# Backward attention: the token-major K, Q and dO of the next group are requested in four column pieces of 64 KB each instead of one piece of 256 KB

## The chip, the cores and the metric

One core of a Trainium2 chip runs the whole kernel. The metric is the time of one execution on the device in microseconds (us), taken as the median over several executions; less is better. The kernel before has a median of 2633.72 us over 6 runs, which lie between 2625.1 and 2644.07 us. One further thing is needed to read the profile: it is taken from a single execution, and everything in it is counted from the start of that execution's span.

## The reference, cut to what matters

The kernel computes a transformer block (layer norm with modulation, softmax attention with 32 heads of 16 columns over 2048 tokens, a squared-ReLU MLP) and the gradients of all its inputs. The change lies in the backward pass of the attention alone. For one head, the forward pass is

```python
scores = jnp.einsum('bhqd,bhkd->bhqk', q, k) * scale
p = _softmax(scores, axis=-1)
o = jnp.einsum('bhqk,bhkd->bhqd', p, v)
```

and its backward pass, with dO the gradient that arrives at o, needs for each head P = softmax(QK^T) again, dP = dO V^T, dS = P * (dP - rowsum(dO * o)), and then dV = P^T dO, dK = dS^T Q and dQ = dS K. Everything is in bfloat16 with float32 accumulation.

## The kernel before, in words

The program has three stretches: the forward pass with the MLP and its gradients, the backward attention (`attn_bwd`, from L1335), and a last phase (`phase6`) with the remaining weight gradients. The backward attention is the middle one that matters here.

**Groups, halves, slots.** The 32 heads are handled as 8 groups of 4 heads (loop over `g`, L1434). Each group has two halves of 2 heads, which the code calls pairs (loop over `jp`, L1435). A half runs over 4 chunks of 512 keys (`c`) and, in each, over 16 blocks of 128 queries (`ib`), in steps of four blocks (`ib0`, L1452). Such a step of four blocks is called a slot here: its number in the half is `m` (L1453), 0 to 15, so there are 16 slots in a half and 256 in all.

**What a block does.** For each of the two heads, TensorE computes a score tile `st` (L1468), ScalarE takes its exponential into `pu` (L1472), TensorE computes `dp` (L1408) and VectorE multiplies both into `ds` (L1410). `kv` (L1365) accumulates dK and dV from `ds`, `pu` and the group's token-major Q and dO. For dQ the tile `ds` has to be transposed. Of the 32 squares of 128x128 in a slot, TensorE turns the first four (L1427, copied to `dsT` by ScalarE at L1428), and one DMA transpose, issued on SyncE's queue at L1418 when the slot's last `ds` is ready, turns the other 28. `dq` (L1387) multiplies `dsT` with the group's token-major K. It is called two blocks at a time, some two slots behind: it starts on a slot when more than 8 blocks are waiting (L1480). There are four `dsT` buffers and three `ds` buffers.

**What a group loads.** A group needs five tensors of its own, kept in two sets of buffers that alternate: QT and dOT (feature-major) and K, Q and dO (token-major, 128 partitions by 1024 columns, that is 2 KB in each partition and 256 KB in all). `load_group(g)` (L1304) makes the list of copies for them, the *pieces*; from group 2 on QT and dOT come in four pieces each (16 rows of 4 KB, 64 KB; 18 rows of 4 KB, 72 KB), for group 1 in two of 256 KB each. `pair_pieces` (L1327) makes four more for each half: the rows of K and V of the two heads of the next half (two of 64 KB, two of 72 KB). Group 0's pieces are issued before the backward attention starts, on SyncE's queue (L908), followed there by the four copies of `WmT`, which only `phase6` reads.

**When a piece is issued.** While group g is computed, GpSimd's queue issues the pieces of group g+1. The first half takes the four pieces of its own second half and the first half of the list of `load_group`, the second half takes the four of the next group and the rest (L1441 to L1444):

```python
pieces = self.pair_pieces(g, 1) + later[:len(later) // 2]
later = later[len(later) // 2:]
...
pieces = self.pair_pieces(g + 1, 0) + later
```

They are spread evenly over the 16 slots, each behind a copy of one element of the last `ds` (`tick`), which holds GpSimd back until the kernel has come that far (L1454 to L1457):

```python
while pieces and (total - len(pieces)) * SC * ST <= m * G * total:
    if last:
        nc.gpsimd.tensor_copy(tick[:], last[7][0:1, 0, 0, 0:1])
    nc.gpsimd.dma_start(*pieces.pop(0))
```

For the groups 2 to 7 the list of `load_group` has 4 + 4 + 3 = 11 pieces. So a first half issues 4 + 5 = 9 pieces (K and V of the next half, the four of QT, one of dOT), in the slots 0, 2, 4, 6, 8, 9, 11, 13 and 15. A second half issues 4 + 6 = 10 (K and V, three of dOT, then K, Q and dO whole), in the slots 0, 2, 4, 5, 7, 8, 10, 12, 13 and 15: the three pieces of 256 KB are the last three. For group 1 the list has 7 pieces, and the halves issue 7 and 8. The order of the instructions on TensorE, SyncE and GpSimd is the order of the code in this stretch (a manual schedule).

Of the kernel before, what the change touches and what calls it, by code (L numbers as in the profile page):

```python
# [25 lines left out]
def chunks(total, size):  # L26
    out = []
    s = 0
    while s < total:
        w = min(size, total - s)  # L30
        out.append((s, w))
        s += w
    return out
# [72 lines left out]
class K:  # L106
# [1197 lines left out]
    def load_group(self, g):  # L1304

        S, ST, qp = self.S, self.ST, self.qp
        tm = {"K": self.ktm_d, "Q": self.qtm_d, "dO": self.dOp_d}
        fm = {"QT": (self.QTq_d, DH), "dOT": (self.dOTq_d, DH + 2)}
        w = ST * 4 * DH
        if g < 2:  # L1310
            T, o = {}, 0
            for n in (*fm, *tm):
                e = S if n in fm else w
                T[n] = self.q0[:, o:o + e] if g == 0 else qp.tile([P, e], BF16, name=f"{n}g")[:]
                o += e
            self.Tq[g] = T
        T, pieces = self.Tq[g % 2], []
        for n, (src, rows) in fm.items():
            if g < 2:
                pieces += [(T[n][:, s0:s0 + sw], src[g, :, s0:s0 + sw]) for (s0, sw) in chunks(S, 1024)]  # L1320
            else:
                pieces += [(T[n][r:r + rows, :], src[g, r:r + rows, :]) for r in range(0, P, 32)]
        for n, src in tm.items():
            pieces.append((T[n], src[g]))
        return {n: t if n in fm else t.rearrange("p (st w) -> p st w", st=ST) for n, t in T.items()}, pieces

    def pair_pieces(self, g, jp):  # L1327
# [422 lines left out]
```

## Time and profile before

| | us |
|---|---|
| median of 6 runs | 2633.72 |
| lowest and highest | 2625.1, 2644.07 |
| the profiled execution | 2627.91 |
| its span, first to last instruction | 2626.1 |
| backward attention in it, from 1180 to 2490 us | 1310 |

| busy in the span | us | share |
|---|---|---|
| TensorE, matmuls (PE) | 2481.5 | 94% |
| ScalarE (ACT) | 2296.2 | 87% |
| VectorE (DVE) | 1769.6 | 67% |
| GpSimd (POOL) | 513.6 | 20% |

How to read the lines that follow in the prediction: PE is TensorE, PEld its weight load, DVE VectorE, ACT ScalarE, POOL GpSimd, and SPq SyncE's queue. A row of the windows gives a stretch (from:to, us), its length, then each engine's busy us with its number of instructions, the clock that TensorE was granted as a share of full speed, the mean busy share of the 16 DMA engines (packets overlap, so it can exceed 1) and GB/s. A row of the waits says who sat idle until what was done: total us, how often, longest. A row of the DMA queues gives the packets, the MB and the time that the packets took as a share of 16 engines; q1 carries what SyncE issues (here the transposes), q0 what GpSimd issues (here the pieces). A row of the DMA issues gives destination and source, queue, number, KB each and the median us from issue to landing.

### The profile page before, as it was taken

How to read it: one execution, taken by the hardware profiler on the slowest of the kernel's cores; microseconds unless marked ns; L12 is line 12 of the kernel's file. 1: busy time of each engine (PE TensorE's matmuls, PEld its weight loads, DVE VectorE, ACT ScalarE, POOL GpSimd, SP SyncE). 2: the span in 40 equal slices, each digit the busy share in tenths (PEclk: the TensorE clock that was granted, in tenths of full speed). 3: DMA queues.
4: the chain of work that ended last, by engine and by line, in shares of the span. 5: the costliest groups of instructions: out<-in, count | busy, mean ns of one | idle time of the engine just before them, and what ended most of it. 6: DMA issues, size and time to landing. Idle time of an engine off the chain costs nothing.

```text
span 2626.1 us, 77231 instructions
## 1 busy us (share of the span) xinstructions
PE 2481.5 (94%) x31005; PEld 1227.2 (47%) x31233; DVE 1769.6 (67%) x3679; ACT 2296.2 (87%) x3712; POOL 513.6 (20%) x965
## 2 busy tenths in 40 slices
PE   8999899999999999899999999999999999998998
PEld 4555555555555554743434344444443444443443
DVE  6222223323423335659999999999999999998867
ACT  7999999999999995319989999999998999998823
POOL 3545511310321131450000000000000000000031
PEclk9999999999999999999999999999999999999999
DMA  5588742520541246999999999999999999999986
GB/s 165 119 184 189 171 81 95 134 66 22 156 100 43 89 104 187 188 238 187 200 188 194 200 184 194 194 193 201 191 193 190 190 200 196 194 195 197 199 224 169
DMA packets 1192126, 433.47 MB, mean 165 GB/s; under 512 B 1136036, under 2 KB 1158054, under 8 KB 1191766
## 3 DMA queue, kind: packets, MB, share of 16 engines
q1 hardware_dynamic: 1154966, 322.79, 71.8%
q0 software_dynamic: 36800, 105.74, 14.4%
q8 instruction: 244, 4.00, 0.6%
q14 instruction: 116, 0.95, 0.1%
HBM read 75.57 MB, written 68.69 MB: 55 GB/s over the span
## 4 chain that ended last, share of the span: by engine, by line
PE 32%; DMA 23%; ACT 2%; issue 2%; SPq 0%; POOL 0%; DVE 0%; POOLq 0%; ACTq 0%
DMA dsT<-ds 22%; PE st L1468 11%; PE acckv L1365 6%; PE accq L1387 5%; PE dps L1002 2%; ACT pu L1472 2%; PE dps L951 1%; PE dp L1408 1%; PE g3ps L1574 1%; PE dxhps L1549 1%; DMA dqT<-dq_t 1%; PE st L1427 1%; DMA du_blk<-duT_d 1%; PE st L1376 1%; PE gps L1599 0%
## 5 line engine op out<-in xcount | busy, mean ns | idle before, releaser
L1410 DVE TENSOR_TENSOR ds<-dp,pu 128x512 bf16<-128x512 f32 x2048 | 1240.6, 678 | 61.3 <-PE dp L1408 54.3
L1472 ACT ACTIVATE pu<-st 128x512 bf16<-128x512 f32 x2048 | 1081.6, 614 | 124.4 <-PE dp L1408 66.8
L382 ACT ACTIVATE pu<-st 128x1024 bf16<-128x1024 f32 x992 | 912.0, 1078 | 4.5 <-PE st L379 4.1
L379 PE MATMUL st<-QTm,KTq 128*128 128x512 bf16 x1859 | 561.4, 377 | 26.8 <-ACT pu L382 6.0
L313 PEld LDWEIGHTS <-pu 128*128 128x128 bf16 x8192 | 346.8, 96 | 236.0 <-issue 2.8
L1387 PEld LDWEIGHTS <-dsT 128*128 128x128 bf16 x8192 | 245.2, 96 | 268.5 <-issue 207.6
L313 PE MATMUL accbank<-Vaug,pu 128*128 128x17 bf16 x8192 | 358.0, 171 | 8.2 <-ACT Vaug L502 1.1
L1408 PE MATMUL dp<-m,q 64*128 64x512 bf16 x1024 | 342.5, 385 | 0.7 <-DMA WmT<-WmT_d 0.7
L1408 PE MATMUL dp<-m,dOTg 64*128 64x512 bf16 x1024 | 341.5, 384 | 0.0
L1468 PE MATMUL st<-m,q 64*128 64x512 bf16 x1024 | 321.3, 384 | 7.7 <-ACT pu L1472 5.4
L1468 PE MATMUL st<-m,QTg 64*128 64x512 bf16 x1024 | 319.8, 384 | 5.0 <-ACT pu L1472 3.1
L379 PEld LDWEIGHTS <-KTq 128*128 128x128 bf16 x1984 | 188.4, 96 | 177.3 <-issue 126.7
L1456 POOL COPY tick<-ds 1x1 bf16<-1x1 bf16 x142 | 25.1, 176 | 1136.4 <-DVE ds L1410 1136.4
L1387 PE MATMUL accq<-q,dsT 128*128 128x16 bf16 x4096 | 150.2, 171 | 26.8 <-DMA dsT<-ds 26.2
L1387 PE MATMUL accq<-Kg,dsT 128*128 128x16 bf16 x4096 | 150.0, 171 | 26.1 <-DMA dsT<-ds 25.6
L1365 PE MATMUL acckv<-ds,Qg 128*16 128x512 bf16 x1024 | 155.5, 383 | 0.3 <-DVE ds L1410 0.2
L1365 PE MATMUL acckv<-ds,q 128*16 128x512 bf16 x1024 | 155.2, 383 | 0.0
L1365 PE MATMUL acckv<-pu,q 128*16 128x512 bf16 x1024 | 155.2, 384 | 0.0
L1365 PE MATMUL acckv<-pu,dOg 128*16 128x512 bf16 x1024 | 155.1, 383 | 0.0
L1428 ACT COPY dsT<-st 128x512 bf16<-128x512 bf16 x256 | 152.4, 595 | 1.1 <-PE st L1427 1.0
L293 POOL DMA_DIRECT2D QTm<-QTq_d x124 | 63.3, 512 | 335.5 <-PE st L379 314.8
L320 DVE RECIPROCAL rl<-accbank 128x4 f32<-128x4 f32 x128 | 22.9, 179 | 152.9 <-PE accbank L313 152.8
(343 smaller groups left out, 2756.9 us busy)
## 6 DMA issues: line engine op xcount, KB each, us to landing
KTq<-KTq_d POOLq DMA_DIRECT2D x24, 512.0 KB, 3.7
duT_d<-auT POOLq DMA_DIRECT2D x4, 1792.0 KB, 8.8
aT_d<-rT POOLq DMA_DIRECT2D x4, 1792.0 KB, 13.9
KTq_d<-KTq SPq DMA_DIRECT2D x32, 128.0 KB, 2.4
QTq_d<-ev_fm SPq DMA_DIRECT2D x32, 128.0 KB, 2.8
VTq_d<-vT POOLq DMA_DIRECT2D x4, 1024.0 KB, 6.4
O_d<-O POOLq DMA_DIRECT2D x4, 1024.0 KB, 6.4
dsT<-ds SPq DMA_TRANSPOSE x256, 7.8
```

Source lines behind the costliest of these rows:

```text
L293: nc.gpsimd.dma_start(QTm[j][32 * j:32 * j + 32, :], self.QTq_d[g, 32 * j:32 * j + 32, 512 * qc:512 * (qc + 1)])
L313: nc.tensor.matmul(acc[:, a, sub, :], lhsT=pu[:, a, sub * P:(sub + 1) * P], rhs=Vaug[:, kb, h, :], start=(kb == 0 and a == 0 and sub == 0) ...
L379: nc.tensor.matmul(stt[:, a, :], lhsT=KT[:, kb * P:(kb + 1) * P], rhs=QTm[2 * jp + a][:], start=True, stop=True)
L382: nc.scalar.activation(pu[:], stt[:], ACT.Exp, scale=self.scale)
L1002: nc.tensor.matmul(pt[:], lhsT=a[:, st, :], rhs=g_tm[:, st, :], start=(st == 0), stop=(st == ST - 1))
L1365: nc.tensor.matmul(acckv[r:r + DH, :], lhsT=T[n][:, ib, col:col + DH], rhs=src[:, a, :], start=(ib == 0), stop=(ib == ST - 1))
L1387: nc.tensor.matmul(accq[:, ib, a, :], lhsT=dsT[:, (i * 2 + a) * 4 + sub, :], rhs=T["K"][:, 4 * c + sub, col:col + DH], start=(c == 0 and i ...
L1408: nc.tensor.matmul(dp[:], lhsT=T["dOT"][rd, ib * P:(ib + 1) * P], rhs=masked["VT"][2 * jp + a][rd, 512 * c:512 * (c + 1)], start=True, sto ...
L1410: nc.vector.tensor_tensor(dsg[:, i, a], dp[:], pu[:, a, :], ALU.mult)
L1428: nc.scalar.copy(dsT[:, 0:4, :], tp[:])
L1468: nc.tensor.matmul(stt[:], lhsT=T["QT"][rs, q], rhs=masked["KT"][2 * jp + a][rs, c0:c0 + 512], start=True, stop=True)
L1472: nc.scalar.activation(pu[:, a, :], stt[:], ACT.Exp, scale=self.scale)
```

## The change

In `load_group`, each of K, Q and dO is no longer one piece but four, cut along the columns. A piece is 128 partitions by 256 columns, that is 512 B in each partition of the destination and in each row of the source (whose rows stay 2 KB apart), 64 KB in all. One such piece holds four of the 16 token blocks.

```diff
         for n, src in tm.items():
-            pieces.append((T[n], src[g]))
+            pieces += [(T[n][:, a:a + w // 4], src[g, :, a:a + w // 4]) for a in range(0, w, w // 4)]
```

The rest follows from the loop that spreads the pieces. The list of the groups 2 to 7 grows from 11 to 20 pieces, and its middle moves: the first half of a group now issues 4 + 10 = 14 pieces (K and V, four of QT, all four of dOT, two quarters of K) and the second half 4 + 10 = 14 (K and V, two quarters of K, four of Q, four of dO), both in the slots 0, 2, 3, 4, 5, 6, 7, 8, 10, 11, 12, 13, 14 and 15. For group 1 the list grows from 7 to 16 and the halves issue 12 each. Group 0's list grows by the same nine, on SyncE's queue. In all GpSimd issues 63 copies more, each with its one-element `tick`, and SyncE 9 more. Bytes, matmuls and the order of the instructions on TensorE stay as they were.

## The prediction

> **What bounds the kernel now.** I read the chain of waits first: which resource ends last.
>
> ```profile
> DMA dsT<-ds 22%; PE st L1468 11%; PE acckv L1365 6%; PE accq L1387 5%; PE dps L1002 2%; ACT pu L1472 2%; PE dps L951 1%; PE dp L1408 1%; PE g3ps L1574 1%; PE dxhps L1549 1%; DMA dqT<-dq_t 1%; PE st L1427 1%; DMA du_blk<-duT_d 1%; PE st L1376 1%; PE gps L1599 0%
> 1180.00:2490.00 1310.00, 1246.91 (x17600) 534.06 (x17597) 1248.18 (x2063) 1230.42 (x2431) 99.26 (x284) 0.99 1.17 194
> ```
>
> The transpose `dsT` holds 22% of the chain, all of it in the backward attention. The second row is that stretch: TensorE, VectorE and ScalarE are each busy for about 1240 of 1310 us and the DMA share is 1.17. Three engines and the DMA are almost equally full, so a late transfer has little to hide behind. Next the waits of that stretch, then DMA windows of two moments: one transpose with no piece beside it, and one with the 256 KB of Q beside it.
>
> ```profile
> PE accq L1387 <- DMA dsT<-ds: 50.9, 60, 4.6
> ```
>
> ```profile
> q1 hardware_dynamic: 3618, 0.92, 118.4%
> ...
> q1 hardware_dynamic: 1039, 0.27, 74.4%
> q0 software_dynamic: 73, 0.24, 47.8%
> ```
>
> The first q1 row is 1220 to 1224.56 us: 3618 packets (one transpose is 28 squares x 128 rows = 3584) in 4.56 us, against a slot that takes 4.78 us when nothing waits (1333.59 to 1338.37 us, all engines busy throughout). A transpose therefore leaves about 0.2 us of its slot free. The other two rows are 1318 to 1322.5 us: beside Q only 1039 packets pass in 4.5 us. The stage is limited by transposes that arrive late once a piece has been among them; `dq` waits 50.9 us for them.
>
> Where do these waits lie? In the slots 10 to 13 of a second half, where K and Q and then dO are requested, the same row reads, for the groups 0 to 6:
>
> ```profile
> PE accq L1387 <- DMA dsT<-ds: 3.4, 1, 3.4
> ...
> PE accq L1387 <- DMA dsT<-ds: 4.6, 1, 4.6
> ```
>
> shows groups 0 and 4; all seven are 3.4, 2.0, 2.3, 2.4, 4.6, 1.6, 2.0, together 18.3 us. The same slots of the first halves give 0.5 + 0.3 + 0.9 + 0.4 = 2.1 us. So 16.2 us belong to the 21 pieces of 256 KB. The whole halves of group 1:
>
> ```profile
> 1348.20:1427.60 79.40, 77.48 (x1106) 33.55 (x1098) 77.92 (x130) 76.52 (x154) 6.05 (x18) 1.00 1.17 196
> 1427.60:1509.40 81.80, 77.45 (x1110) 33.14 (x1109) 77.77 (x129) 77.41 (x154) 6.94 (x20) 1.00 1.20 195
> ```
>
> VectorE works 77.8 us in either half; the second is 2.4 us longer.
>
> **The change part by part.** *Removed: the 256 KB bursts.* If none of their waiting stays, -16.2 us. Long waits cost a little more: after the 3.4 us of group 0 the slot 1326.76 to 1333.59 us ran at a granted clock of 0.65. The two slots from 1319.48 to 1333.59 us together took 14.11 instead of 9.56, 4.55 more for a wait of 3.4, so 1.1 on top. I leave that to the range.
>
> *Added: 84 pieces of 64 KB* (12 for each of the groups 1 to 7). A small piece is not free: the first halves of groups 1 to 6 wait 0.9 + 4.6 + 3.1 + 2.3 + 2.1 + 1.1 = 14.1 us with 54 pieces, mostly of 64 to 72 KB, 0.26 us each. The slots 0 to 9 of the second halves wait 1.8 + 0.5 + 0.3 + 0.7 + 0.4 + 0.2 = 3.9 us with 42 such pieces, 0.09 us each. Ten of the twelve new pieces fall into second halves, two into first: (10 x 0.09 + 2 x 0.26) / 12 = 0.12 us each, 84 x 0.12 = +10.1 us. Upper bound: all at 0.26, and each packet dearer because its runs are 512 B. For that I compare 512 KB copies of GpSimd's queue with short and longer runs: the store of `dOTq` (512 B runs, 739 to 745 us), then that of `xhat` (1 KB rows, 795 to 801 us).
>
> ```profile
> q0 software_dynamic: 144, 0.52, 29.6%
> ...
> q0 software_dynamic: 144, 0.52, 21.4%
> ```
>
> 29.6 / 21.4 = 1.38 for the same bytes, so 0.26 x 1.38 = 0.36 us and 84 x 0.36 = +30.2 us. These are stores and the pieces are loads, so it is a bound and not my value. Lower bound: nothing, if the pieces fit the free 0.2 us of their slots.
>
> *Moved: three pieces of dOT* per group from the second to the first half (groups 2 to 7): 3 x (0.26 - 0.09) x 6 = +3.1 us; lower bound 0.
>
> *GpSimd:* 63 more copies with ticks.
>
> ```profile
> POOL tick L1456 <- DVE ds L1410: 1136.4, 142, 17.9
> L1457 POOL DMA_DIRECT2D Kg<-ktm_d x4: 551/562/565, 1304.5 to 2294.3; - x4
> ```
>
> 63 x (0.18 for the tick + 0.29 between + 0.55) = 64 us of a queue that waits 1136 us for `ds`. That waiting hides them; queued behind a tick are only later pieces. Were the cover gone, pieces would land late. The nearest deadline is the first quarter of dO, issued in slot 12 and read after slot 15; the landing of whole dO takes 6.3 us (issue rows), three slots are 14 us. The last quarter is issued in slot 15 and read in slot 3. Cost 0.
>
> *SyncE:* nine more issues of 0.43 to 0.57 us before group 0, 4 to 5 us. They delay `WmT`, read only in the last phase, and then the first transpose at 1185.16 us; SyncE was idle from 1170.6 us. Each issue also waits for the copy eight before it, whose landing takes 4 to 5 us, which could move the end of the list to about 1177 us, still 8 us early. Cost 0; without the cover, up to +5.
>
> **Sum:** -16.2 + 10.1 + 3.1 = -3.0 us. The span of 2626.1 becomes 2623.1. The median lies 7.6 us above that span; with this added, 2631 us.
>
> **A rule that speaks against the change.** The page "DMA: Bandwidth & Descriptors" of the Trainium skill, section "Rules for kernel authors", says to coalesce small transfers into a large one, since under 64 KB one pays mostly overhead. Its table in "Bandwidth" has 0.95 us of DMA time for 64 KB and 6.15 us for 1 MB; along a straight line 256 KB would be 1.99 us, so quarters would cost 4 x 0.95 - 1.99 = 1.8 us more for each tensor, an estimate from that page, 38 us for 21 tensors if all of it reached the path. The trace is nearer to neutral: the windows above give 0.09 to 0.26 us of waiting for a small piece and 16.2 / 21 = 0.77 for a large one.
>
> **The rivals.**
>
> *Faster, the pieces fit.* Cut in four, no piece is longer than what two slots leave free, so the waits of 16.2 us go and the new pieces cost next to nothing; the clock stays up (-1.1). 2633.7 - 17 = 2617 us. For it: the wait of the second halves before slot 10 is only 0.09 us per piece. Against it: the first halves, where 64 KB pieces in neighbouring slots do wait.
>
> *Slower, every occupied slot waits.* A transpose fills 4.56 of 4.78 us, so a stage that gets a piece in 28 of 32 slots instead of 19 never catches up. At 0.36 us: -16.2 + 30.2 + 3.1 = +17, 2651 us. The point from which it decides: (16.2 - 3.1) / 84 = 0.16 us for a new piece is break-even, 0.31 us brings a loss of 13 us. For it: the 0.26 us of the first halves and the factor 1.38. Against it: the second halves.
>
> *It changes nothing.* The same bytes take the same DMA time and the waiting only moves. 2634 us. For it: the DMA share is the same in halves with and without large pieces (1.17 to 1.20). Against it: beside Q the total falls to 112 GB/s (1318 to 1322.5 us) from 201 in the window without a piece, so bursts do lose time, not only move it.
>
> **How the numbers follow.** About 0.5%, 13 us, is what a measurement of this kernel can tell from no change; the six runs spread by 19. My sum and "nothing" give one answer, within 0.5%: 0.43 together (0.31 and 0.12). "Fits" gets 0.28: 17 us is just over the bound. "Every slot waits" gets 0.29, since its price rests on rows one step away. The likeliest is the sum, 2631 us; its own range is 2620 (new pieces at nothing: -16.2 + 3.1 = -13) to 2642 (new pieces at 0.26 us: -16.2 + 21.8 + 3.1 = +9). For 8 in 10 I go to the far rivals at either side, with the spread of a median of some runs: 2610 to 2652.
>
> **What would show it.** In the trace after, the slots 10 to 13 of the second halves should wait about as long as those of the first halves, with no single wait over 2 us; if waits of 3 to 4 us remain, the burst was not the cause. The total of `accq` waiting for `dsT` should fall from 50.9 to about 48; 35 means "fits", 65 or more means "every slot waits". The first halves of groups 2 to 7 should grow by about 0.8 us each, the second shrink by 1.0. GpSimd's ticks should still wait over 1000 us, and the first transpose should still be issued near 1185 us. I am wrong in kind if something new waits: TensorE at L1365 for a quarter of Q or dO, or GpSimd for an earlier piece.

## The result, and the profile after

The changed kernel takes 2616.05 us (median of 29 executions, 2602.48 to 2630.95). The kernel before, measured beside it, takes 2633.88 us (66 executions, 2619.39 to 2649.05). The ratio is 0.9932 with a 95% interval of 0.9919 to 0.9946: the change makes the kernel 0.68% faster, 17.8 us. That lies inside the stated range of 2610 to 2652 us, and it is the rival "the pieces fit" (2617 us, given 0.28). The likeliest case of the prediction, 2631 us, had the direction but only 3 of the 17.8 us.

The same views as before, in the same order. First the chain of waits of the changed kernel:

```profile
DMA dsT<-ds 18%; PE st L1468 13%; PE acckv L1365 7%; PE accq L1387 6%; PE dps L1002 2%; ACT pu L1472 2%; PE dp L1408 2%; PE dps L951 1%; PE st L1427 1%; PE g3ps L1574 1%; PE dxhps L1549 1%; DMA dqT<-dq_t 1%; DMA du_blk<-duT_d 1%; PE st L1376 1%; PE gps L1599 0%
```

The transpose gave up 4 points of the chain (22% to 18%), and TensorE's own lines (`st`, `acckv`, `accq`) took them. No new resource appears in it. The waits of the stretch from 1180 to 2490 us (who waited for what: total us, how often, longest us):

```profile
POOL tick L1456 <- DVE ds L1410: 1065.4, 205, 19.4
...
PE accq L1387 <- DMA dsT<-ds: 40.3, 53, 3.8
```

`dq` waits 40.3 us for transposes instead of 50.9. The two windows do not end alike: the last transpose is issued at 2488.1 us before and at 2475.6 after, so only the second window holds the waits behind it. Counted from the first to the last transpose, it is 38.5 us instead of 50.9. GpSimd still stands 1065 us before `ds`, so its 63 additional copies did stay under cover. The same waits in the slots 10 to 13 of the second halves follow. As in the prediction, the slots of a wait are counted by the half's transposes; a piece that the loop puts into its slot m is issued about two transposes earlier. In the second half of group 1 of the kernel before, K, Q and dO, which the loop has in its slots 12, 13 and 15, are issued 10.2, 11.3 and 13.3 transposes into the half. There is one answer for each of the groups 0, 1, 2, 4, 5 and 6 (group 3 has none):

```profile
PE accq L1387 <- DMA dsT<-ds: 0.8, 1, 0.8
...
PE accq L1387 <- DMA dsT<-ds: 0.6, 1, 0.6
...
PE accq L1387 <- DMA dsT<-ds: 1.8, 2, 1.0
...
PE accq L1387 <- DMA dsT<-ds: 0.3, 1, 0.3
...
PE accq L1387 <- DMA dsT<-ds: 0.6, 1, 0.6
...
PE accq L1387 <- DMA dsT<-ds: 0.5, 1, 0.5
```

The sum is 4.6 us, against 18.3 before, and no wait is longer than 1.0 us. The DMA queues of the changed kernel from 1319.5 to 1324 us, a moment with a quarter of dO beside a transpose (packets, MB, share of 16 engines):

```profile
q1 hardware_dynamic: 3512, 0.89, 115.1%
q0 software_dynamic: 32, 0.07, 8.7%
```

Beside the whole Q, 1039 packets of transposes passed in 4.5 us. Beside this quarter 3512 pass, almost the 3584 of one transpose. Five other windows of 4.5 us beside a quarter of dO hold 2322 to 3692; some contain a pause in which hardly anything moves, but none is as slow as beside Q.

Now the halves. A row of the windows is from:to, length, busy us (and instructions) of PE, PEld, DVE, ACT, POOL, then clock, DMA share, GB/s. Group 4 of the kernel before, first and second half:

```profile
1837.00:1917.40 80.40, 77.47 (x1104) 33.41 (x1096) 77.71 (x130) 76.66 (x153) 6.08 (x18) 1.00 1.21 195
1917.40:2002.10 84.70, 78.70 (x1110) 33.64 (x1112) 78.25 (x130) 77.17 (x154) 6.91 (x20) 0.98 1.16 190
```

Groups 1 and 4 of the changed kernel:

```profile
1348.40:1430.60 82.20, 78.62 (x1106) 33.13 (x1104) 78.37 (x130) 77.22 (x153) 9.58 (x28) 0.98 1.19 195
1430.60:1512.30 81.70, 78.85 (x1110) 33.47 (x1112) 78.16 (x130) 77.34 (x154) 9.90 (x28) 0.98 1.15 192
1833.70:1914.00 80.30, 77.52 (x1112) 33.45 (x1104) 77.97 (x130) 76.93 (x153) 9.57 (x28) 1.00 1.20 199
1914.00:1994.40 80.40, 77.00 (x1101) 33.37 (x1096) 77.36 (x129) 76.51 (x152) 9.89 (x28) 1.00 1.23 195
```

In group 4 the second half lost 4.3 us and became as long as the first. GpSimd's column shows the additional pieces: 28 instructions instead of 18 and 20. Group 1 shows why no single half should be read: its two halves are no shorter than before (81.7 against 81.8 for the second), and both ran at a clock of 0.98. One profile moves by several us from half to half, so the table has further profiles of both kernels (b2, a2 and a3 below), and the text uses the means.

Five profiles, in us. "Stage" is from the first to the last transpose `dsT`, "waits" is `accq` waiting for `dsT` in it (a row of waits whose window ends later has up to 2.3 us more), "slots 10–13" is the part of it in those slots of the second halves of groups 0 to 6. The halves are means over groups 1 to 6. "Lost clock" sums, over the stretches of the stage in which the clock was 0.50, half of their length. The last column is TensorE's busy time in the stage.

| | span | stage | waits | slots 10–13 | first half | second half | lost clock | TensorE busy |
|---|---|---|---|---|---|---|---|---|
| before | 2626.1 | 1302.9 | 50.9 | 18.2 | 80.6 | 82.1 | 10.2 | 1240.2 |
| before again (b2) | 2632.2 | 1314.5 | 55.4 | 18.8 | 80.9 | 83.5 | 22.6 | 1246.8 |
| change | 2612.4 | 1292.1 | 38.5 | 4.6 | 80.9 | 80.1 | 8.5 | 1240.2 |
| change again (a2) | 2620.0 | 1289.8 | 37.8 | 1.3 | 81.4 | 79.4 | 6.8 | 1238.5 |
| change, third (a3) | 2609.7 | 1292.2 | 40.0 | 2.7 | 81.6 | 80.0 | 6.8 | 1239.0 |

The mean stage goes from 1308.7 to 1291.4 us. These 17.3 us are about the 17.8 of the medians, so no part outside the backward attention is needed; that they agree so closely is partly luck, since the two profiles of the kernel before differ by 11.6 us. The waits give 53.2 - 38.8 = 14.4 of them. TensorE's busy time for the same matmuls gives 1243.5 - 1239.2 = 4.3, but nearly all of that comes from b2: the first profiles of the two kernels have the same 1240.2. Against it, `st` waits 1.6 us longer for `pu` (means 7.0 and 8.6).

### The profile page after: what moved, and what is told of

Its sections match the earlier page's. It is cut to its first block, busy times and chain, and to the rows that moved or that the text cites. A ratio compares the mean times of both kernels' runs of the same rounds, so it can differ in the third digit from the quotient of the medians.

```text
span 2612.4 us, 77500 instructions
## 1 busy us (share of the span) xinstructions
PE 2477.8 (95%) x31005; PEld 1225.7 (47%) x31233; DVE 1769.3 (68%) x3679; ACT 2296.3 (88%) x3712; POOL 558.5 (21%) x1091
## 4 chain that ended last, share of the span: by engine, by line
PE 35%; DMA 20%; ACT 2%; issue 2%; SPq 0%; POOL 0%; DVE 0%; POOLq 0%; ACTq 0%; DVEq 0%
DMA dsT<-ds 18%; PE st L1468 13%; PE acckv L1365 7%; PE accq L1387 6%; PE dps L1002 2%; ACT pu L1472 2%; PE dp L1408 2%; PE dps L951 1%; PE st L1427 1%; PE g3ps L1574 1%; PE dxhps L1549 1%; DMA dqT<-dq_t 1%; DMA du_blk<-duT_d 1%; PE st L1376 1%; PE gps L1599 0%
## 5 line engine op out<-in xcount | busy, mean ns | idle before, releaser
L1456 POOL COPY tick<-ds 1x1 bf16<-1x1 bf16 x205 | 36.2, 176 | 1065.4 <-DVE ds L1410 1065.4
```

## The experiments

### Both kernels again: what the clock does after a long wait

The kernel before, once more, to see how far its own profile can be trusted:

> The kernel before once more, for a second profile. Its first profile is of an execution of 2627.9 us, 6 us under its median of 2633.9, and has 1302.9 us from the first to the last transpose of ds, 11.5 us more than the mean of three profiles of the change (1291.4), while the medians differ by 17.8 us. If the first profile was a short one of this stage, it takes 1305 to 1312 us here with 53 to 58 us of waits of accq for dsT, and the stage explains the whole difference. If the rest lies elsewhere, it takes 1301 to 1304 us again, and something outside the stage is longer than in the profiles of the change.

It took 2634.01 us in its one execution. Its stage is 11.6 us longer than in the first profile with waits only 4.5 us longer, and TensorE busy for 6.6 us longer; the windows around one of its long waits show where this lies. First the waits from 1290 to 1320 us:

```profile
PE accq L1387 <- DMA dsT<-ds: 4.1, 3, 3.6
```

Then three windows of the same kernel, of which the first holds that wait (columns as above, the third from the right is TensorE's clock):

```profile
1304.00:1312.20 8.20, 5.32 (x76) 2.20 (x73) 6.52 (x11) 5.99 (x12) 0.00 (x0) 1.00 1.26 146
1312.20:1319.00 6.80, 5.83 (x60) 1.80 (x60) 3.38 (x6) 3.61 (x7) 0.72 (x2) 0.50 1.07 222
1319.00:1326.00 7.00, 6.75 (x104) 2.86 (x100) 6.72 (x12) 6.51 (x14) 0.00 (x0) 1.00 0.94 143
```

After the wait the clock is 0.50 for 6.8 us. In these 6.8 us TensorE does 60 matmuls, against 104 in the 7.0 us that follow, and VectorE is busy for half of the time. This comes on top of the wait.

A shorter wait can do it too. In the changed kernel a wait of 1.4 us ends at 1389.4 us; the wait, then three windows:

```profile
PE accq L1387 <- DMA dsT<-ds: 1.4, 1, 1.4
```

```profile
1387.90:1391.10 3.20, 1.80 (x30) 0.74 (x30) 1.96 (x5) 2.30 (x5) 0.00 (x0) 1.00 1.23 254
1391.10:1394.50 3.40, 3.40 (x36) 1.02 (x32) 2.88 (x6) 2.93 (x6) 0.69 (x2) 0.50 1.14 184
1394.50:1397.90 3.40, 3.40 (x59) 1.49 (x56) 3.02 (x6) 2.89 (x6) 0.50 (x2) 1.00 1.30 187
```

At 0.50 there are 36 matmuls in 3.4 us, then 59. Over the five profiles, all 9 waits of `accq` of 3 us or more were followed by a stretch at 0.50, of 3.4 or 6.8 us; so were 12 of the 25 waits of 1.25 to 2 us, always for 3.4 us, 3 of the 5 of 2 to 3 us, and only 4 of the 250 under 1.25 us. The Trainium skill, page "TensorE: Matmul & The Clock Gate", part 1, "What's actually happening", has the clock at half rate after at least one idle window of about 3.4 us. The waits of 3 us and more agree with that; those of 1.25 to 2 us do not, and here the measurement decides.

Of the stretches at 0.50 in the stage, 3 of 5 in the first profile of the kernel before and 5 of 10 in b2 begin in the slots 10 to 13 of the second halves of groups 0 to 6. With the change none does (11 stretches in three profiles), and there no wait in these slots is over 1.0 us. The lost clock is not simply added to the waits: 14.4 us of waits and 9.0 us of clock (means 16.4 and 7.4) together would exceed the 17.3 us. What reaches the stage of it is at most the 4.3 us of TensorE's busy time.

The change again, twice, on the chips of the later experiments:

> The changed kernel once more, beside the others of this call on one chip. Ratio to before 0.9932 as found, within 0.9915 to 0.995. Its own question: the 48 transposes and loads ahead of the backward attention (from the first transpose of du to the first of a) took 92.0 us in the profile of before and 85.9 us in that of the change, and no instruction there differs. If that is chance from run to run, it will lie anywhere from 84 to 97 us here; if it belongs to the kernel, at 86 us.

> The changed kernel as a yardstick for the two others of this call. Ratio to before 0.9925 to 0.9955; waits of accq for dsT 39 to 41 us; first to last transpose of ds 1289 to 1293 us.

Measured: 2622.22 us, ratio 0.9950 [0.9932, 0.9969], and 2616.68 us, 0.9939 [0.9916, 0.9962]. The waits of the stage in a2:

```profile
PE accq L1387 <- DMA dsT<-ds: 39.2, 56, 3.7
```

and in a3:

```profile
PE accq L1387 <- DMA dsT<-ds: 41.7, 61, 3.2
```

So the gain and its place hold in three profiles. Whether a chip gives 0.5 or 0.7% is within the intervals.

### The parts of the change

The change does two things at once: it cuts the copies, and it moves pieces between the halves. The first four experiments take them apart and set a floor.

**e1, the quarters in the old halves.** On the changed kernel, the list is cut where it was cut before (4 of QT and one of dOT in the first half). The second line lets the last slot issue what is left, since a half now has over 16 pieces.

```diff
-pieces = self.pair_pieces(g, 1) + later[:len(later) // 2]
-later = later[len(later) // 2:]
+cut = (5 if g else 3) if g + 1 < NQ else len(later) // 2
+pieces = self.pair_pieces(g, 1) + later[:cut]
+later = later[cut:]
...
-while pieces and (total - len(pieces)) * SC * ST <= m * G * total:
+while pieces and ((total - len(pieces)) * SC * ST <= m * G * total or m == SC * ST // G - 1):
```

> K, Q and dO in quarters, but the list is cut where it was cut before: the first half of a group issues K and V, four of QT and one of dOT (9), the second half three of dOT, all twelve quarters and K and V of the next (19, so three slots issue two). Theory 'burst' (a 256 KB copy among the transposes costs more than its quarters do one by one): most of the gain stays, ratio to before 0.993 to 0.995, waits of accq for dsT some 40 to 43 us. Theory 'room' (the gain is that the second half has fewer bytes to carry, since dOT moved to the first): the gain is gone, ratio 0.998 to 1.002, second halves again about 82 us each.

**e2, whole pieces in the new halves.** On the kernel before, QT and dOT are all in the first half and K, Q and dO, whole, have the second for themselves.

```diff
-pieces = self.pair_pieces(g, 1) + later[:len(later) // 2]
-later = later[len(later) // 2:]
+cut = (8 if g else 4) if g + 1 < NQ else len(later) // 2
+pieces = self.pair_pieces(g, 1) + later[:cut]
+later = later[cut:]
```

> K, Q and dO whole (256 KB), but all of QT and dOT in the first half, so the second half issues only K and V of the next and the three large pieces, in slots 0, 3, 5, 7, 10, 12 and 14. Burst: each large piece still costs its 0.8 us of waiting, ratio 0.998 to 1.001, waits 48 to 52 us, single waits of 3 us or more remain. Room: nearly the whole gain, ratio 0.993 to 0.995.

**e3, no token-major pieces.** As e2, but K, Q and dO are loaded for the groups 0 and 1 alone. This leaves out work that the result needs: the later groups compute with the K, Q and dO that lie in the two sets of buffers.

```diff
-pieces.append((T[n], src[g]))
+if g < 2:
+    pieces.append((T[n], src[g]))
```

> Left out: K, Q and dO of the groups 2 to 7 are not loaded at all (the two sets of buffers keep those of the groups 0 and 1, the output is not the reference's); QT and dOT all in the first half. This is the floor: what all 18 large pieces cost together, against the run with the same halves and whole pieces. Burst: whole pieces cost about 1 us each, quarters nearly nothing, so the floor lies at or just under the changed kernel: ratio 0.990 to 0.993. If quarters cost 0.12 us each as I had it (72 x 0.12 = 9 us), the floor lies 9 us under the changed kernel: ratio 0.989 to 0.990. Room: also 0.990, but then the whole pieces with the new halves are as fast as the change.

**e4, quarters by rows.** The same 64 KB, cut along the partitions, so that each row keeps its 2 KB.

```diff
-pieces.append((T[n], src[g]))
+pieces += [(T[n][r:r + 32, :], src[g, r:r + 32, :]) for r in range(0, P, 32)]
```

> Quarters of 64 KB again, but cut by partitions (32 partitions by 2 KB each, source contiguous) and not by columns (128 partitions by 512 B). Slots and halves as in the changed kernel. If runs of 512 B cost more (the factor 1.38 of the stores), this is faster than the change: ratio 0.989 to 0.991. If only the size of a piece matters, it is the same: 0.992 to 0.995. If what matters is that a piece lies evenly over all partitions, it is slower than the change: 0.996 or more.

| | us | ratio, 95% | stage | waits | slots 10–13 |
|---|---|---|---|---|---|
| e1 | 2616.68 | 0.9945 [0.9922, 0.9967] | 1297.5 | 43.1 | 4.7 |
| e2 | 2630.22 | 0.9987 [0.9963, 1.0012] | 1314.4 | 58.9 | 13.4 |
| e3 | 2607.63 | 0.9917 [0.9886, 0.9948] | 1288.6 | 38.4 | 2.4 |
| e4 | 2624.56 | 0.9983 [0.9959, 1.0006] | 1294.3 | 40.8 | 2.7 |

e1 and e2 settle which part it is. Cutting alone gives the gain, within the intervals; moving alone gives none that can be measured. The waits of e2's stage:

```profile
PE accq L1387 <- DMA dsT<-ds: 58.9, 63, 5.0
```

Whole pieces keep their long waits (5.0 us the longest) wherever the others are put. e3 is the floor. Its 18 whole pieces less than e2 are worth 2630.22 - 2607.63 = 22.6 us, 1.26 us each; the two intervals leave some 10 us on either side of the 22.6. And its waits are

```profile
PE accq L1388 <- DMA dsT<-ds: 40.3, 48, 3.0
```

as long as those of the changed kernel (38.4 us of them in the stage, against 38.8). So waiting of this size is there without any K, Q and dO of the groups 2 to 7. In the time, the floor lies 9.0 us under e1, which ran beside it, and 4.0 under the change by the two ratios; with an interval of 8 us on either side it cannot tell these from nothing.

e4 looked like a contradiction. Its stage is like the change's (1294.3, with 2.7 us in the slots 10 to 13), but its time is not. Its trace differs elsewhere: the stage ahead, between the first transposes of `du_blk` and of `a_blk`, took 96.8 us, where e1, e2 and e3 have 83.5 to 89.4 us and the instructions are the same. It was measured again, beside the change.

> The quarters by rows once more. In its first profile the backward attention was as short as with the change (1294.3 us from first to last transpose of ds, the change 1292.1, before 1302.9), but the stage ahead of it, from the first transpose of du to the first of a, took 96.8 us. If that is chance, the ratio to before now comes down to that of the change, 0.992 to 0.995. If it belongs to this kernel, the ratio stays at 0.997 to 0.999 and the stage near 97 us.

Measured: 2623.2 us, 0.9952 [0.9930, 0.9975], and a2 beside it 0.9950. Its stage is 1292.1 us. So in the backward attention both profiles of e4 are like the change, and in the second measurement so is the time. The first, 0.9983 over 12 executions, stays unexplained: one profile with a long stage ahead does not show that the other executions had one too. That the cut by columns costs more, by its 512 B in each row, is not seen in either.

**e5, every quarter twice.** On the changed kernel, from group 1 on, each quarter is requested a second time: 84 more pieces of 64 KB, which is the marginal price by itself.

```diff
-pieces += [(T[n][:, a:a + w // 4], src[g, :, a:a + w // 4]) for a in range(0, w, w // 4)]
+for a in range(0, w, w // 4):
+    pieces += [(T[n][:, a:a + w // 4], src[g, :, a:a + w // 4])] * (2 if g else 1)
```

(with the second condition of e1 in the loop)

> The price of a quarter by itself: for the groups 1 to 7 each of the twelve quarters is requested twice in a row (the same bytes to the same place), so 84 copies of 64 KB come on top and some slots issue two. Burst with a low price (0.05 us each, as the floor without token-major loads says): 84 x 0.05 = +4 us on the change, ratio to before 0.994 to 0.996. My price of 0.12 us: +10, ratio 0.997. The price of the first halves, 0.26 us: +22, ratio 1.001 or more.

Measured: 2626.48 us, 0.9969 [0.9949, 0.9990]; the change beside it took 2622.22. The difference is 4.3 us for 84 pieces, 0.05 us each. The two intervals together leave about 7 us on either side, so the price lies between nothing and 0.14 us: below the break-even of 0.16, but 0.12 is not excluded. Its one profile is less kind:

```profile
PE accq L1388 <- DMA dsT<-ds: 59.0, 65, 4.0
```

These 59.0 us are 20 more than in a2, beside it, with 20 pieces in the 16 slots of a half, so that some slots have two; they are not all a slot apart. That execution (2633.75 us) was slower than this kernel's median by 7 us. So the times leave the price of a quarter open between nothing and 0.14 us. How the waits of a half grow with its number of pieces, over all runs, is in the next section.

**e7, halves instead of quarters** (`w // 4` becomes `w // 2`, 128 KB each).

> K, Q and dO in two pieces of 128 KB each. If the cost grows with the length of a piece (burst), half of the gain or a bit more: ratio 0.994 to 0.997. If a piece only has to fit into what one or two slots leave free, 128 KB already does: 0.9925 to 0.994, the same as quarters. If it doesn't fit, no gain: 0.998 or more.

Measured: 2615.13 us, 0.9927 [0.9900, 0.9953], stage 1294.8, waits in it 40.1. As good as the quarters.

**e9, four quarters in one slot.** Is it the size of a copy, or how much is requested at once? On the kernel before, each of K, Q and dO of the groups 1 to 7 is cut in four copies, but all four are issued behind one `tick`, in the slot that issued the whole.

```diff
-pieces.append((T[n], src[g]))
+pieces.append([(T[n][:, a:a + w // 4], src[g, :, a:a + w // 4]) for a in range(0, w, w // 4)])
...
-nc.gpsimd.dma_start(*pieces.pop(0))
+p = pieces.pop(0)
+for d in (p if isinstance(p, list) else [p]):
+    nc.gpsimd.dma_start(*d)
```

(group 0's copies stay whole)

> For the groups 1 to 7 K, Q and dO are again one entry of the list each, in the slots and halves of the kernel before, but an entry is issued as its four quarters one right after the other (one tick for the four). If a long copy as such holds the transposes up (size), the gain is there: ratio 0.992 to 0.996. If it is 256 KB between two transposes, however cut (spacing), there is no gain: 0.998 to 1.001, and the slots 10 to 13 of the second halves wait some 15 to 20 us in the groups 0 to 6, as before (18.2), not 1 to 5 us as with the change.

Measured: 2630.0 us, 0.9994 [0.9975, 1.0013], no gain at all. Waits of its stage:

```profile
PE accq L1390 <- DMA dsT<-ds: 51.1, 53, 3.8
```

In the slots 10 to 13 they are 15.8 us, and 17.1 us are lost to the clock: the kernel before again. The second half of group 3 shows both in a row (windows of e9, columns as above):

```profile
1826.00:1829.00 3.00, 0.09 (x3) 0.09 (x4) 0.17 (x1) 0.00 (x0) 0.00 (x0) 1.00 1.04 126
...
1829.90:1833.30 3.40, 3.40 (x38) 1.08 (x36) 2.58 (x4) 2.46 (x5) 2.28 (x5) 0.50 1.22 253
```

For 3 us the compute engines stand still (TensorE 0.09 us busy) while the DMA works at 126 GB/s, and then TensorE runs at half clock for 3.4 us. So it is not the size of a copy. It is 256 KB requested at one place among the transposes, in whatever copies; spread over four or over two slots the same bytes cost little. This is the experiment that decides: its interval lies clear of that of the change, and e1 has the same quarters in the same halves, spread. How the DMA engines divide their time between the two queues is not shown by it.

**e8, the other large pieces too.** What is left of 256 KB or more on this queue: QT and dOT of group 1, and the loads for the last phase that group 7 issues (`A_wqkv`, `xhat`). All are cut to 128 KB.

```diff
-... for (s0, sw) in chunks(S, 1024)]
+... for (s0, sw) in chunks(S, 512 if g else 1024)]
...
-later = [(self.wq_6[:, kt, :], self.io["A_wqkv"][kt * P:(kt + 1) * P, :]) for kt in range(self.DT)]
+later = [(self.wq_6[:, kt, a:a + D], self.io["A_wqkv"][kt * P:(kt + 1) * P, a:a + D])
+         for kt in range(self.DT) for a in range(0, 3 * D, D)]
...
-pieces = [(self.xhat1_6[:, st:st + 2, :], ...[:, st:st + 2, :]) for st in range(0, ST, 2)]
+pieces = [(self.xhat1_6[:, st, :], ...[:, st, :]) for st in range(ST)]
```

> The change, and the other long copies of this stage cut too: QT and dOT of group 1 in four of 128 KB each (not two of 256 KB), the last loads of A_wqkv in six of 128 KB (not two of 384 KB) and those of xhat in sixteen of 128 KB (not eight of 256 KB). With the change the first half of group 0 waits 5.4 to 6.8 us, the halves of group 7 some 5 us each, against 2.1 to 3 us in the first and 0.8 to 1.5 us in the second halves between. If long copies are the cause there too, these waits fall by about 8 us in all: ratio to before 0.990 to 0.992, and 4 to 9 us under the changed kernel of this call. If the cause there is the beginning and end of the stage, no difference to the change.

Measured: 2610.78 us, 0.9917 [0.9886, 0.9948], with a3 beside it at 2616.68. Its stage is 1288.7 us, and the longest wait is down to 2.1 us:

```profile
PE accq L1387 <- DMA dsT<-ds: 38.4, 56, 2.1
```

It has the lowest median of the kernels that compute everything, but its interval overlaps that of the change, so the further 5.9 us are not shown.

## Why the prediction was right in direction and wrong in size

**The removed bursts, -16.2: right.** The waits in the slots 10 to 13 of the second halves went from 18.2 and 18.8 to 4.6, 1.3 and 2.7 us (means 18.5 and 2.9, -15.6). The total of the waits in the stage, 38.8 us on average, lies between the 48 of the sum and the 35 of "fits", nearer to "fits".

**The added quarters, +10.1: this step failed.** It took the waits that the halves already had, divided them by the pieces that they already had, and charged each new piece this mean (0.26 and 0.09 us). With the +3.1 for the moved dOT, at the same means, the stage should then have waited 13.2 us longer outside the slots 10 to 13 of the second halves. It waited 32.7 and 36.6 us there before, and 33.9, 36.5 and 37.3 after: 1.2 us longer on average. A mean wait is not what one more piece costs, and the halves show it:

| waits of groups 1 to 6, us | pieces in a half | in the profiles of |
|---|---|---|
| first halves: 14.1, 14.0, 13.7, 14.8 | 9 | before, b2, e1, e9 |
| first halves: 20.3, 18.2 | 12, none a quarter | e2, e3 |
| first halves: 12.9, 18.0, 17.2 | 14, two of them quarters | change, a2, a3 |
| first halves: 21.8 | 20 | e5 |
| second halves: 3.6 | 4 | e3 |
| second halves: 8.8, 4.9, 8.7 | 14, ten of them quarters | change, a2, a3 |
| second halves: 14.2, 13.4 | 19, 20 | e1, e5 |

From 9 to 14 pieces in the six first halves, 30 more, the means rise by 1.9 us, 0.06 for each; 0.26 would have been 7.8. From 4 to 14 in the second halves, 60 more, they rise by 3.9 us, again 0.06. From 14 to 19 or 20, where some slots have two, it is more. The sums scatter by some 5 us between profiles of one kernel, so 0.06 is an estimate: it is small against 0.26, but the times of e5 alone cannot tell it from 0.12. The factor 1.38 for short runs, read from stores, did not show in the loads (the rows of e4 were not faster than the columns).

The prediction's lower end, "if the pieces fit the free 0.2 us of their slots", was nearer, and its reading of the free time was too narrow. The row of DMA rates of its own window without a piece, 1220 to 1224.56 us in 40 slices, is

```profile
GB/s 25 159 220 209 220 162 112 38 9 9 11 9 9 18 258 292 290 290 290 290 287 290 294 287 287 296 292 287 292 290 290 278 274 274 269 265 243 241 70 23
```

In seven neighbouring slices, 0.8 us, the DMA moves 38 GB/s or less. The 4.56 us are not filled by the transpose. How much of such a pause a piece can use is not shown.

**The halves.** The first became 0.55 us longer on average (80.75 to 81.3), against +0.8 predicted; the second became 3.0 us shorter (82.8 to 79.8), against 1.0. The slots 0 to 9 of the second halves waited 3.9 and 5.1 us before and 4.3, 2.8 and 5.9 after, with 9 pieces issued in them instead of 6. The price of the moved dOT, +3.1, stays open. The first halves of e2 and e3, which have three pieces of dOT more than before and no quarter, wait 4 to 6 us longer, about the 18 x 0.26 = 4.7 of the prediction; with the change, which moves the same pieces, they wait only 2.0 longer on average; and e1, which does not move them, is no faster than the change.

**The clock, left to the range: right as a small term.** The prediction saw one long wait with 1.1 us on top and put it aside. Half or more of the stretches at half clock of the kernel before began in the slots of the removed waits; what the clock was worth in the stage is at most the 4.3 us of TensorE's busy time, and these rest on b2.

So of the 14.3 us between the forecast of -3.0 and the measured -17.3 of the stage, 11.4 are waits (-14.4 instead of -3.0), nearly all of them the charge for the added and moved pieces; the other 2.9 are about what TensorE's shorter busy time leaves after the longer waits for `pu`.

**GpSimd and SyncE at 0: right.** GpSimd's ticks wait 1065.4 us, and the waits of the changed kernel have no row of TensorE waiting for a quarter of Q or dO. The first transpose is issued at 1183.5, 1191.7 and 1179.5 us with the change and at 1185.2 and 1178.2 us without: nine more issues on SyncE are not seen among the spread of the stage ahead.

**The rule to coalesce** would have made the change 38 us dearer, by the estimate from the page "DMA: Bandwidth & Descriptors". The runs show the reverse, -17.8 us, and in e9 three more copies for each tensor, issued together, are neither a gain nor a loss that can be measured (0.9994). The rule concerns the time of a copy; here the time of a copy lies under other work, and what counts is how long the transposes beside it are held up.

**The rivals.** "Every slot waits" decides from 0.16 us for a piece; e5 has at most 0.14. "It changes nothing", the waiting only moves, falls with the total of the waits. One stretch did get longer, which I had not foreseen: the first half of group 0 lasts 84.2, 83.5 and 83.6 us with the change, 78.4 and 82.7 before. The change gives it a copy of 256 KB of dOT and four quarters of K more, but e1, where it has its old pieces, has 85.0, so these are not shown to be the cause. In e8, which cuts the copies of 256 KB there as well, it lasts 79.4 us, which one profile does not settle either.

## What to carry to other kernels

A mean wait per piece is not a price per piece: before charging an added transfer with it, compare stretches with fewer and with more of them, and run the floor that leaves them out. Where a stream of transfers paces the work, request other data in small portions spread along it; here 64 or 128 KB a slot apart did it, and four copies of 64 KB issued together gained nothing. And look at the clock behind each long wait on TensorE: in these profiles it was halved after every wait of 3 us or more and after about half of those of 1.25 to 2 us.

## What the hardware showed unexpectedly

A quarter takes about as long to land as a whole tensor: the issues of the changed kernel (destination and source, queue, count, KB each, median us to landing)

```profile
Kg<-ktm_d POOLq DMA_DIRECT2D x16, 64.0 KB, 6.4
```

and 6.2 to 6.7 us for the other quarters of K, Q and dO that GpSimd issues, against 4.9 to 8.6 us for the whole tensors before. Beside the transposes the landing time says little about the size of a copy, or about what it costs the others.

The stage ahead varied from 82.6 to 96.8 us between the profiled executions, with the same instructions. That is nearly as much as the whole effect. Its cause was not looked for, and whether it made e4 look like no gain in its first measurement is not shown. Open, too, is why 40 us of waits remain with no K, Q or dO of the groups 2 to 7 in the queue; the pieces of QT, dOT, K and V of the halves are left as candidates, and none was taken out by itself.
